# Layout of the filter loads, queue assignment, norm by reciprocal square root, and E±O on VectorE in a spectral mixer kernel

## The chip, the cores and the metric

The kernel runs on one core of one Trainium2 chip. The metric is device time in microseconds (us), the median of several runs. Runs carry a state, fast or slow, and only fast runs are compared. The engines are called PE (TensorE; PEld is its weight load), DVE (VectorE), ACT (ScalarE), POOL (GpSimd) and SP (SyncE, which here only issues loads and stores). Line numbers such as L714 are those of the kernel that the profile belongs to, so the same operation has another number before and after.

## The reference, cut to what matters

```python
# x: 1 x 2048 x 512 bf16; w_r, w_i: 2048 x 257; w1: 2048 x 1376; w2: 1376 x 2048
h  = x + irfft2(rfft2(layernorm(x)) * (w_r + 1j * w_i))     # "A": a spectral filter
g  = layernorm(layernorm(h))                                # B norms its input again
u  = gelu(einsum("bsd,sf->bdf", g, w1) + b1)
y  = einsum("bdf,fs->bds", u, w2) + b2
out = h + transpose(y)
```

Both Fourier transforms are done as matmuls. The kernel runs through four stages: A, norm of x and the first transform over the rows (matmuls of X with F, the matrix F scaled by 1/std first, because the norm can be folded into the matrix); B, the filter in 16 chunks c (matmul with E, matmul with L, multiply P with the filter, matmul with H); C, the inverse transform in 16 blocks, each normed and at once fed into six of the eleven row tiles of the first layer, then the other five tiles; D, the second layer and the stores.

## The kernel before

The program is not written instruction by instruction. Every operation is entered with the pieces of memory that it reads and writes. A builder notes, per 32-byte cell of a partition's memory, who wrote and who read it, makes the dependencies from that, and a list scheduler then fixes the order on each engine. This is the function that turns an access into cells; `lo` is the tensor's place in a partition, `ap.ap` lists (step, count) per dimension, the first being the partition:

```python
CELL = 32
def cells_of(self, ap):
    lo = self.tensors[ap.tensor.name]
    esz = dt.size(ap.dtype)
    gran = CELL if lo < (1 << 20) else 256
    offs = np.array([int(ap.offset)], dtype=np.int64)      # <- includes start partition * pitch
    for step, n in list(ap.ap)[1:]:
        ...
    b = lo + offs * esz
    return np.unique(...)                                  # cell numbers
```

The filter loads: three pieces of the frequency range, each cut by component, real or imaginary row, and two more indices, 16 partitions each, half on SyncE's queue, half on GpSimd's; 52 loads in all:

```python
pieces = [(0, 8), (8, 18), (18, 32)]
for pi, (ta, tb) in enumerate(pieces):
    for comp, wsrc in enumerate((A_w_r, A_w_i)):
        q = "sp" if comp == 0 else "pool"
        ...  # for reim, j, sgn: p0 = 4 * j + 2 * sgn + reim
            dma(f"ld_w{comp}_{pi}_{p0}_{a}", q, W[p0:NP:8, a:b, comp, :], src, ...,
                group=f"W{pi}{q}", wgroup=f"W{pi}")
K.op("mk_eps", "dve", lambda e, eng: eng.memset(eps[:, 0:1], LN_EPS), outs=[eps[:, 0:1]], ...)
```

The norm and the inverse, cut:

```python
K.op(f"sd{g}", "act", ... activation(sd, var, ACT.Sqrt, bias=eps) ...)
K.op(f"rs{g}", "dve", ... reciprocal(rs, sd) ...)
K.op(f"fs{n2}_{s}", ("pool" if g < 7 else "dve"), ... FS[:, n2, 128*s:128*s+128] = F * rs * (1 - 2 s) ...)
...
# inverse block n2: E and O are the halves of eo; result is [E+O, E-O] through one matrix
eng.matmul(ps[:, bA, :] as 2 x 256, IF[:, 0, n2, :], E broadcast twice, start=True, stop=False)
eng.matmul(ps[:, bA, 0:256],   IF[:, 0, n2, :], O, start=False, stop=False)
eng.matmul(ps[:, bA, 256:512], IF[:, 1, n2, :], O, start=False, stop=True)     # IF[:, 1] = -IF[:, 0]
# then DVE: H = ps + X; ACT: square with accumulation, Sqrt; DVE: reciprocal, HH = (H + nm) * A2
```

## Time and profile before

| | |
|---|---|
| time, median of 3 | 176.13 us (175.13 to 176.43) |
| span in the profile | 174.4 us |
| stage A, to the first filter matmul | 49.78 us, of which VectorE is busy in none of the first 31.48 |
| stage B, filter | 26.10 us |
| stage C, inverse with the first six tiles (36.96), other five tiles (20.34) | 57.30 us |
| stage D | 41.2 us |

From the page of the kernel before, the busy shares in 40 slices of 4.36 us (a digit is tenths):

```profile
...
PE   0000000088858999685989889899999999999992
...
DVE  0000000788507786836453455510000333223331
...
POOL 7994000069630100000000000000000000000000
...
DMA  5999987000039999999400000000000011111011
...
```

The first seven slices show loads running at full tilt and no computing engine at work; GpSimd is busy only because its load issues count as work. The chain of waits, followed back from the last instruction (start us, length us, what), has this near its beginning:

```profile
...
0.74 2.70 DMA X<-in_A_x_dram
3.44 28.04 issue
31.48 0.08 DVE st L509
...
```

The first x tile landed at 3.44 us. Then follow 28.04 us of "issue", the name for time in which the engine waited for nothing that the profile could name. The timeline of the start (start, length, engine, line, operation, out<-in, count) shows what ran meanwhile:

```profile
...
1.27 13.98 POOL L459 DMA_DIRECT2D W<-in_A_w_i_dram  x26 [0.82 <-POOLq L825]
...
7.82 21.22 SPq L459 DMA_DIRECT2D W<-in_A_w_r_dram  x26
31.48 0.69 DVE L509 BATCH_NORM_STATS2 st<-X 128x6 f32<-128x512 bf16 x1 [31.48 <-issue]
31.50 0.06 DVE L499 MEMSET eps<- 128x1 f32 x1
...
```

The memset of `eps` needs no data at all and yet ran at 31.5 us. (The record of the first statistics starts 0.02 us before the memset's; by its operands it waits for x alone, which had landed at 3.44 us, so it seems to have stood behind the memset in VectorE's queue.) The operands in the trace say that the memset waits on a semaphore, and that this is the semaphore of the last group of SyncE's filter loads, whose last landing is at 31.45 us. SyncE issues those 26 loads in 21.22 us. What that holds up is told by the list of waits of the whole kernel (waiting engine, its tile and line, what it waits for: us in total, times, longest):

```profile
...
PE ps L535 <- POOL FS L521: 36.3, 3, 35.5
...
ACT junk L501 <- DVE eps L500: 27.9, 1, 27.9
...
```

The stages of the kernel before in the view by stretches (stretch, length, then busy us and count of instructions for PE, PEld, DVE, ACT, POOL, then granted TensorE clock, DMA share, GB/s):

```profile
...
0.00:49.78 49.78, 11.49 (x65) 7.57 (x65) 13.30 (x50) 11.28 (x18) 24.06 (x58) 1.00 0.55 149
49.78:75.88 26.10, 22.78 (x257) 18.88 (x257) 17.89 (x28) 19.44 (x36) 2.69 (x6) 1.00 0.97 371
75.88:112.84 36.96, 32.69 (x191) 17.71 (x196) 17.91 (x45) 23.16 (x61) 0.00 (x0) 1.00 0.25 81
...
```

In the inverse stage TensorE is busy 32.69 of 36.96 us. In the last two stretches it is busy 20.23 of 20.34 and 37.86 of 41.22 us.

### The profile page before, as it was taken

To read this page: it belongs to the slowest core of one execution; us is meant where nothing else is said; L and a number is where in the kernel's file an instruction comes from. 1 tells how busy PE (TensorE), PEld (TensorE's weight loads), DVE (VectorE), ACT (ScalarE), POOL (GpSimd) and SP (SyncE) were. 2 spreads that over 40 slices of the span, in tenths; PEclk is the share of its full clock that TensorE was granted. 3 is DMA by queue.
4 is the path that set the end of the run, shared out by engine and by line. 5 is a ranking of instruction groups with operands and counts; after the bars stand their busy time and mean duration, and the time that the engine had idled before them with its cause. 6 is when DMAs were issued, how large, how long until landed. Compare 5 with 4: busy or idle time off the path is not lost.

```text
span 174.4 us, 2045 instructions
## 1 busy us (share of the span) xinstructions
PE 125.1 (72%) x775; PEld 78.9 (45%) x784; DVE 62.4 (36%) x142; ACT 63.2 (36%) x130; POOL 26.7 (15%) x64
## 2 busy tenths in 40 slices
PE   0000000088858999685989889899999999999992
PEld 0000000055637978553545445444446666666661
DVE  0000000788507786836453455510000333223331
ACT  2000000136778787647467664695121000000000
POOL 7994000069630100000000000000000000000000
PEclk9999999999999999999999999999999999999999
DMA  5999987000039999999400000000000011111011
GB/s 136 311 315 283 274 202 167 14 0 0 2 96 294 406 421 411 421 357 305 192 0 0 0 0 4 0 0 0 0 4 0 30 60 60 60 64 57 33 60 62
DMA packets 13322, 22.23 MB, mean 127 GB/s; under 512 B 1792, under 2 KB 9120, under 8 KB 13184
## 3 DMA queue, kind: packets, MB, share of 16 engines
q1 hardware_dynamic: 11392, 19.21, 32.3%
q0 software_dynamic: 1200, 2.11, 5.1%
q10 hardware_dynamic: 720, 0.79, 1.5%
q8 instruction: 6, 0.10, 0.2%
q14 instruction: 4, 0.03, 0.1%
HBM read 20.00 MB, written 2.10 MB: 127 GB/s over the span
## 4 chain that ended last, share of the span: by engine, by line
PE 62%; issue 18%; ACT 8%; DVE 8%; DMA 2%; POOL 1%; DVEq 0%
PE ps L751 20%; PE ps L714 19%; PE ps L535 5%; PE ps L623 4%; PE ps L589 4%; PE ps L680 3%; DVE H L695 2%; ACT Y L546 2%; PE ps L689 2%; PE ps L572 2%; ACT SQ L698 2%; DMA X<-in_A_x_dram 2%; ACT Xsb L598 1%; PE ps L757 1%; DVE HH L706 1%
## 5 line engine op out<-in xcount | busy, mean ns | idle before, releaser
L714 PE MATMUL ps<-HH,W 128*128 128x512 bf16 (+1 forms) x171 | 40.8, 379 | 4.1 <-DVE A L704 2.1
L535 PE MATMUL ps<-FS,X 128*128 128x256 bf16 x64 | 11.5, 357 | 36.7 <-POOL FS L521 36.3
L751 PE MATMUL ps<-GT,W 128*128 128x512 bf16 (+1 forms) x162 | 35.7, 379 | 0.2
L751 PEld LDWEIGHTS ps<-GT,W 128*128 128x128 bf16 (+1 forms) x165 | 23.8, 144 | 11.9
L763 DVE SCALAR_TENSOR_TENSOR OUT<-ps,B2f,H 128x512 bf16<-128x512 f32 x16 | 12.0, 751 | 44.6 <-PE ps L751 24.4
L714 PEld LDWEIGHTS ps<-HH,W 128*128 128x128 bf16 (+1 forms) x176 | 17.0, 100 | 20.9 <-issue 4.0
L535 PEld LDWEIGHTS ps<-FS,X 128*128 128x128 bf16 x64 | 7.6, 125 | 40.3 <-POOL FS L521 37.3
L509 DVE BATCH_NORM_STATS2 st<-X 128x6 f32<-128x512 bf16 x16 | 10.2, 669 | 31.5 <-issue 31.5
L698 ACT ACTIVATE SQ<-H,nm 128x512 bf16<-128x512 bf16 x16 | 11.5, 717 | 9.4 <-DVE H L695 9.4
L459 POOL DMA_DIRECT2D W<-in_A_w_i_dram x26 | 14.0, 551 | 0.8 <-POOLq L825 0.8
L695 DVE TENSOR_TENSOR H<-ps,X 128x512 bf16<-128x512 f32 x16 | 10.9, 689 | 7.7 <-PE ps L692 7.7
L521 POOL TENSOR_SCALAR FS<-F,rs 128x128 bf16<-128x128 bf16 x28 | 9.9, 372 | 21.3 <-DVE mv L511 21.1
L605 DVE TENSOR_TENSOR P<-Xsb,W 128x1024 bf16<-128x1024 bf16 x16 | 10.6, 685 | 5.5 <-ACT Xsb L598 5.4
L684 ACT ACTIVATE EO<-ps 128x512 bf16<-128x512 f32 x16 | 9.1, 585 | 5.1 <-PE ps L680 5.1
L733 ACT ACTIVATE GT<-ps,B1f 128x512 bf16<-128x512 f32 (+1 forms) x11 | 6.9, 695 | 10.9 <-PE ps L714 10.8
L598 ACT ACTIVATE Xsb<-ps 128x512 bf16<-128x512 f32 x16 | 9.4, 596 | 3.1 <-PE ps L589 3.1
L589 PE MATMUL ps<-Bsb,Lm 128*128 128x256 bf16 x64 | 9.6, 274 | 1.2 <-ACT Bsb L576 1.2
L623 PE MATMUL ps<-Hm,P 128*128 128x128 bf16 x128 | 9.3, 219 | 1.5 <-DVE P L605 1.3
L501 ACT ACTIVATE junk<-eps 128x1 f32<-128x1 f32 x1 | 0.2, 202 | 27.9 <-DVE eps L500 27.9
L546 ACT ACTIVATE Y<-ps 128x1024 bf16<-128x1024 f32 x8 | 8.1, 1022 | 5.2 <-PE ps L535 5.1
L638 DVE CAST TT<-ps 128x512 bf16<-128x512 f32 x12 | 7.9, 689 | 5.3 <-PE ps L623 5.3
L680 PE MATMUL ps<-GD,TT 128*128 128x256 bf16 x64 | 9.3, 273 | 0.7 <-ACT TT L637 0.7
(37 smaller groups left out, 97.8 us busy)
## 6 DMA issues: line engine op xcount, KB each, us to landing
W<-in_B_w_dram SPq DMA_DIRECT2D x8, 688.0 KB, 13.4
W<-in_B_w_dram SPq DMA_DIRECT2D x10, 512.0 KB, 17.3
out_dram<-OUT SPq DMA_DIRECT2D x16, 128.0 KB, 1.7
X<-in_A_x_dram SPq DMA_DIRECT2D x7, 256.0 KB, 10.2
IF<-c_IF SPq DMA_DIRECT2D x1, 1024.0 KB, 6.0
W<-in_A_w_i_dram POOLq DMA_DIRECT2D x8, 112.0 KB, 6.8
W<-in_A_w_r_dram SPq DMA_DIRECT2D x8, 112.0 KB, 3.1
W<-in_A_w_i_dram POOLq DMA_DIRECT2D x8, 80.0 KB, 6.3
```

Source lines behind the costliest of these rows:

```text
L459: return eng.dma_start(dst, src)
L535: r = eng.matmul(ps[:, b, 256 * u:256 * u + 256].rearrange("p (a b) -> p a b", a=2), X[:, n2, 128 * t:128 * t + 128], fr if t < 2 else fa, ...
L546: return eng.activation(dst, src, ACT.Copy)
L589: r = eng.matmul(ps[:, b, 256 * h:256 * h + 256], Lm[:, v, m, :], Bs[:, 256 * m:256 * m + 256], start=(h == 0 and m == 0), stop=(h == 1 an ...
L598: return eng.activation(dst, src, ACT.Copy)
L623: r = eng.matmul(o, P[:, h, m, par::2], Hm[:, v, m, :], start=(c % 2 == 0 and h == 0 and m == 0), stop=(c % 2 == 1 and h == 1 and m == 1), ...
L680: r = eng.matmul(o, TT[:, q, n2, par, :], GD[:, par, q, :], start=(i == 0), stop=(i == 3), skip_group_check=True)
L695: K.op(f"h{n2}", "dve", lambda e, eng: eng.tensor_tensor(H[:, n2, :], ps[:, bA, :], X[:, n2, :], ALU.add), ins=[ps[:, bA, :], X[:, n2, :]] ...
L698: K.op(f"sq{n2}", "act", lambda e, eng: eng.activation(sq[:, :], H[:, n2, :], ACT.Square, bias=nm[:, n2, 0:1], accum_out=s2t[:, n2, 0:1]), ...
L714: return eng.matmul(ps[0:Mt, bank, :], W1[:, n2, 128 * t:128 * t + Mt], HH[:, n2, :], start=(n2 == 0), stop=(n2 == 15), skip_group_check=True)
L751: r = eng.matmul(ps[:, b, :], W2[t][0:Kt, n2::16], GT[0:Kt, t, :], start=(t == 0), stop=(t == NFT - 1), skip_group_check=True)
L763: K.op(f"fin{n2}", "dve", lambda e, eng, n2=n2, b=b: eng.scalar_tensor_tensor(OUT[:, n2, :], ps[:, b, :], B2f[:, n2:n2 + 1], H[:, n2, :], ...
```

## The change

Its intent: filter loads of 32 partitions each (28 in place of 52), all on SyncE behind x, so that GpSimd is free for scaling F; F stored with its negative beside it (256 columns) so that one scaling per block does; F's loads on ScalarE's and GpSimd's queues; 1/std in one ScalarE activation (Abs_reciprocal_sqrt) in place of Sqrt and a VectorE reciprocal; statistics of blocks 1 and 3 on ScalarE; in the inverse, E+O and E-O on VectorE for the last 13 blocks and one matmul in place of three, while the first three blocks add x through an identity matrix on TensorE. The matrices L, H, F are permuted to suit the new row order. And, unannounced, the dependency builder is altered: the offset is taken modulo the partition's size, PSUM gets one cell per bank, and two readers of one bank are put in order. The core of the diff:

```diff
 def cells_of(self, ap):
-    gran = CELL if lo < (1 << 20) else 256
-    offs = np.array([int(ap.offset)], dtype=np.int64)
+    gran = CELL if lo < (1 << 20) else PSUM_BANK
+    pitch = int(np.prod(list(ap.tensor.shape)[1:])) * dt.size(ap.tensor.dtype) // esz
+    offs = np.array([int(ap.offset) % pitch], dtype=np.int64)
...
-            wv = wsrc.rearrange("(k2 r) k -> k2 r k", r=NP)
-            q = "sp" if comp == 0 else "pool"
-            (16 partitions: W[p0:NP:8, a:b, comp, :], 52 loads)
+            wv = wsrc.rearrange("(q r) k -> q r k", r=64)
+            (32 partitions: W[2 * ss + reim:NP:4, a:b, comp, :], 28 loads, all on "sp")
...
-    for g in range(4): ld_F on "act", 4 blocks of 128 columns each
+    for g in range(8): ld_F on "act" if g < 2 else "pool", 2 blocks of 256 columns each
...
+    ACT_STATS = (1, 3)                      # x**2 and x summed on ScalarE for these blocks
-    sd = Sqrt(var + eps) on act; rs = reciprocal(sd) on dve; FS in two halves of 128
+    rs = Abs_reciprocal_sqrt(var + eps) on act; FS in one piece of 256
...
+    for lo, hi in ([(0, 2)] if g < 6 else [(0, 1), (1, 2)]):    # last two copies into Y: act and dve
...
-    three matmuls (512 + 256 + 256 columns) per inverse block
+    n2 < 3:  identity matmul of X, then the three
+    n2 >= 3: sd_[:, 0:256] = E + O, sd_[:, 256:512] = E - O on dve; one matmul of 512
```

## The prediction

> **What bounds the kernel now.** The chain of waits begins with 28.04 us of "issue" (3.44 to 31.48 us). The first x tile landed at 3.44 us, yet VectorE starts nothing until 31.48, and TensorE, ScalarE and GpSimd then wait for it (waits: TensorE 35.5 us, ScalarE 27.9). The trace's operands show why: the first VectorE instruction, the memset of eps, which needs no data, waits on the semaphore of the last filter piece, whose last landing is at 31.46. I read this as a false dependency. The dependency builder takes a slice's offset without removing its start partition, so filter slices starting at partition 1 to 7 appear to lie over other tiles, eps among them. The diff's least advertised line, the offset modulo the partition pitch, removes it.
>
> Stages (busy time in stretches): norm and first transform 31.5-49.8 (18.3 us), filter 49.8-75.9 (26.1), inverse plus first matmul 75.9-112.8 (36.9, TensorE busy 32.7), then two TensorE-bound stages to 174.4 (61.6).
>
> **Costs of the change, by stage.**
>
> 1. Start. The norm starts at about 3.5 us instead of 31.5, now under the loads. x and the doubled F are 3.15 MB; at the 0.31 MB/us of the early slices they land by about 12.5 us. VectorE needs 0.8 us per block (0.66 statistics overlapping 0.17 aggregation) for 14 blocks, plus the F scalings given to it (0.25 us for 128 columns now, estimate 0.3 for 256). Two blocks go to ScalarE, which delays the first transform to about 7 us. TensorE there runs cold (213 ns from matmul to matmul, later 109; the Trainium skill, "TensorE: Matmul & The Clock Gate", Part 1, gives half clock until some 3.4 us of activity; the trace agrees in size), 0.83 us a block, about VectorE's pace. So the stage ends near 19 us, not 49.8: about 31 us won. GpSimd's 14.0 us of filter issues were hidden behind the false wait.
>
> 2. Filter stage: same work, 26 us. Its data become the danger: 4.2 MB of filter in 512 B rows, 28 issues on SyncE at 0.6-0.8 us, landing about 20, 25 and 31 us by piece; the multiplies need them at about 21.5, 27 and 34. I expect no large wait.
>
> 3. Inverse stage: 13 blocks replace matmuls of 512+256+256 columns (0.44 us start to end of issue) by one of 512 (0.22): 2.8 us of TensorE less; three identity matmuls add 0.66. VectorE adds two 256-wide additions (estimate 0.25 us each) per block and loses the 0.16 us reciprocals and a hop. Block latency grows to about 4 us, so part is lost in waits. Net about 2.4 us won. Abs_reciprocal_sqrt replaces Sqrt one for one: I expect two table loads as now (1.28 us each). The skill, "ScalarE: Activation LUTs", Table sets, says cheap functions are in every set; were Square not, every block would pay that.
>
> 4. Last stages unchanged. Loads of W1 and W2 queue behind the filter (from about 30 us), landing about 35-60, ahead of need (47 and 100).
>
> **Prediction: 143 us** (176.1 - 30.8 - 2.4), 8 in 10 between 139.5 and 148. Faster by over 2%: 0.98; within: 0.01; slower: 0.01.
>
> **Right if** VectorE's first work is at 3-4 us; the first filter matmul at 18-20.5; filter stage 25-28 us; inverse stage 33-36; rest 61.6.
>
> **Wrong if** another false wait remains; the third filter piece lands after 34 us (multiplies waiting for DMA); the x loads are slowed by the F and filter traffic; ScalarE reloads tables; or the inverse stage stalls on the longer chain.

## The result, and the profile after

The changed kernel takes 144.92 us (median of 4, 143.80 to 145.36) against 176.28 us of the kernel before in the same rounds. The ratio of the means of their fast runs is 0.8229, 95% interval 0.8158 to 0.8301. Ratios in this text are always such: the mean time of one kernel's fast runs over that of the other's of the same rounds, so not quite the quotient of the medians. The measured time lies within the predicted range of 139.5 to 148, 1.9 us above the 143.0. The busy shares in the slices, from the page of the changed kernel:

```profile
...
PE   0059767899996897899999999999999999999991
...
DVE  0469762777788209777777710000032323232322
...
POOL 7238504220000000000000000000000000000000
...
DMA  4999799999999999930000000000011111111111
...
```

The slices are now 3.57 us long. VectorE works from the first slice on, and the loads run beside the work. The timeline of the start of the changed kernel:

```profile
...
0.79 0.06 DVE L498 MEMSET eps<- 128x1 f32 x1 [0.79 <-PEq L861]
...
3.53 0.69 DVE L523 BATCH_NORM_STATS2 st<-X 128x6 f32<-128x512 bf16 x1 [2.56 <-DMA X<-in_A_x_dram]
...
7.88 3.98 SPq L468 DMA_DIRECT2D W<-in_A_w_r_dram  x6
...
8.48 1.89 PE L548 MATMUL ps<-FS,X 128*128 128x256 bf16 x8 [8.48 <-POOL FS L534]
...
```

The memset runs at 0.79 us and the first statistics at 3.53 us, as soon as x is there. TensorE's first matmuls start at 8.48 us, while SyncE has only just begun to issue the filter loads (7.88 us). The stages of the changed kernel in the view by stretches, with the columns as before:

```profile
...
0.00:21.99 21.99, 9.95 (x65) 6.68 (x66) 13.30 (x40) 13.27 (x27) 10.61 (x27) 1.00 0.88 268
21.99:48.08 26.09, 22.77 (x257) 18.85 (x257) 17.89 (x28) 19.44 (x36) 2.81 (x6) 1.00 1.02 364
48.08:81.29 33.21, 31.59 (x171) 16.69 (x172) 21.10 (x56) 23.72 (x61) 0.00 (x0) 0.95 0.43 158
...
```

Beside the lines shown of before: stage A 49.78 to 21.99 us (27.8 won), B 26.10 to 26.09, the inverse stage 36.96 to 33.21 (3.75 won), the rest 61.6 both times. The last number before the DMA share is the granted clock: 0.95 in the inverse stage, which was 1.00 before. That is looked into below. One caution for this column: the clock records begin only at 13.78 us in this trace and at 44.14 us in that of before, and the view prints 1.00 ahead of them. TensorE was not at full pace there: the matmuls of the first transform start 213 ns apart up to these times and 109 ns apart after them. The end of stage A, from the chain of waits:

```profile
...
18.94 0.29 ACT rs L530
19.23 1.89 ACT Y L560 x3
21.12 0.02 issue
21.15 0.70 DVE Y L561
21.85 0.14 issue
21.99 0.61 PE ps L589 x4
...
```

After the last 1/std is known (19.23 us), three copies into Y on ScalarE take 1.89 us, and VectorE's copy of block 15 starts only when they are done. The reader should ask why it waits for ScalarE at all.

The steady part of the inverse stage, from the same kernel's chain of waits (start, length, what):

```profile
...
65.72 1.08 PE ps L748 x5
66.80 0.44 PE ps L702 x4
67.23 0.21 PE ps L748
67.45 0.22 PE ps L724
67.66 1.08 PE ps L748 x5
...
```

TensorE alone, with no other engine in the chain: 6 matmuls of the first layer (L748), four of the inverse's first half (L702), one of its second (L724), 1.95 us a block. Before, the chain passed through VectorE and ScalarE there, for instance in these lines of TensorE's timeline of the kernel before (the bracket gives the idle time ahead of the instruction and what ended it; 0.44 us waiting for VectorE's HH, 0.17 us for ScalarE's EO):

```profile
...
95.75 0.60 PE L680 MATMUL ps<-GD,TT 128*128 128x256 bf16 x4
96.79 1.04 PE L714 MATMUL ps<-HH,W 128*128 128x512 bf16 x4 [0.44 <-DVE HH L706]
...
100.37 0.39 PE L689 MATMUL ps<-EO,IF 128*128 128x512 bf16 x1 [0.17 <-ACT EO L684]
```

### The profile page after: what moved, and what is told of

Read it like the earlier page. It is cut to its first block, busy times and chain, and to the rows that moved or that the text cites. A ratio compares the mean times of both kernels' runs of the same rounds, so it can differ in the third digit from the quotient of the medians.

```text
span 142.9 us, 1989 instructions
## 1 busy us (share of the span) xinstructions
PE 122.9 (86%) x761; PEld 77.1 (54%) x761; DVE 65.7 (46%) x142; ACT 65.7 (46%) x139; POOL 13.4 (9%) x32
## 4 chain that ended last, share of the span: by engine, by line
PE 76%; ACT 8%; DVE 6%; issue 5%; POOL 3%; POOLq 0%
PE ps L748 27%; PE ps L785 25%; PE ps L702 5%; PE ps L640 5%; PE ps L606 5%; ACT Y L560 3%; POOL F L468 2%; PE ps L548 2%; PE ps L589 2%; PE ps L724 2%; ACT Xsb L615 2%; PE ps L791 2%; ACT Bsb L593 1%; ACT SQ L730 1%; POOL FS L534 1%
## 5 line engine op out<-in xcount | busy, mean ns | idle before, releaser
L748 PE MATMUL ps<-HH,W 128*128 128x512 bf16 (+1 forms) x176 | 42.0, 379 | 1.0 <-DVE HH L736 0.9
L785 PEld LDWEIGHTS ps<-GT,W 128*128 128x128 bf16 (+1 forms) x165 | 23.8, 144 | 11.9
L748 PEld LDWEIGHTS ps<-HH,W 128*128 128x128 bf16 (+1 forms) x176 | 17.4, 100 | 19.5 <-issue 1.7
L548 PE MATMUL ps<-FS,X 128*128 128x256 bf16 x64 | 9.9, 320 | 10.3 <-POOL FS L534 10.2
L730 ACT ACTIVATE SQ<-H,nm 128x512 bf16<-128x512 bf16 x13 | 9.4, 722 | 6.7 <-DVE H L726 6.7
L726 DVE TENSOR_TENSOR H<-ps,X 128x512 bf16<-128x512 f32 x13 | 9.0, 691 | 6.2 <-PE ps L724 6.1
L523 DVE BATCH_NORM_STATS2 st<-X 128x6 f32<-128x512 bf16 x14 | 9.1, 672 | 5.7 <-DMA X<-in_A_x_dram 5.7
L702 PE MATMUL ps<-GD,TT 128*128 128x256 bf16 x64 | 10.6, 300 | 1.3 <-ACT TT L654 0.7
L589 PE MATMUL ps<-E,Y 128*128 128x256 bf16 x64 | 8.3, 272 | 1.8 <-DVE Y L561 1.8
L702 PEld LDWEIGHTS ps<-GD,TT 128*128 128x128 bf16 x64 | 6.7, 107 | 5.4 <-ACT EO L706 1.0
L593 ACT ACTIVATE Bsb<-ps 128x512 bf16<-128x512 f32 x16 | 8.7, 603 | 1.5 <-PE ps L589 1.5
L640 PEld LDWEIGHTS ps<-Hm,P 128*128 128x128 bf16 x128 | 7.8, 98 | 2.7 <-DVE P L622 1.8
```

The lines of the kernel that those rows point to most:

```text
L548: r = eng.matmul(ps[:, b, 256 * u:256 * u + 256].rearrange("p (a b) -> p a b", a=2), X[:, n2, 128 * t:128 * t + 128], fr if t < 2 else fa, ...
L589: r = eng.matmul(o, Y[:, k, c, :], E[:, k, :].rearrange("p (h r) -> p h r", h=2), start=(i == 0), stop=(i == 3), skip_group_check=True)
L593: K.op(f"Be{c}", "act", lambda e, eng: eng.activation(Bb[c % 3][:, :], ps[:, b, :], ACT.Copy), ins=[ps[:, b, :]], outs=[Bb[c % 3][:, :]], ...
L640: r = eng.matmul(o, P[:, h, m, par::2], Hm[:, v, m, :], start=(c % 2 == 0 and h == 0 and m == 0), stop=(c % 2 == 1 and h == 1 and m == 1), ...
L702: r = eng.matmul(o, TT[:, q, n2, par, :], GD[:, par, q, :], start=(i == 0), stop=(i == 3), skip_group_check=True)
L730: K.op(f"sq{n2}", "act", lambda e, eng: eng.activation(sq[:, :], hsrc, ACT.Square, bias=nm[:, n2, 0:1], accum_out=s2t[:, n2, 0:1]), ins=[h ...
```

## The experiments

Twelve runs were made, e12 being the changed kernel once more; all gave correct results. Stages are read from each one's profile. "Stage C" is here the time from the first inverse matmul to the first matmul of the second layer, a boundary that is easy to find in every trace (57.30 us before, 53.55 after).

| kernel | time, us | stage A | B | C |
|---|---|---|---|---|
| before | 176.0 to 176.7 | 49.78 | 26.10 | 57.30 |
| after | 144.92; again 144.54 | 21.99; 21.88 | 26.09 | 53.55; 53.47 |
| e1 before, offset modulo pitch | 157.95 | 31.43 | 26.10 | 57.08 |
| e2 after, without the modulo | 169.51 | 47.86 | 26.09 | 53.64 |
| e3 after, three matmuls | 148.86 | 22.23 | 26.09 | 57.80 |
| e4 after, 16-partition loads | 155.13 | 22.24 | 37.61 | 51.98 |
| e5 after, Sqrt and reciprocal | 146.71 | 23.59 | 26.09 | 55.67 |
| e6 after, cells of 16 bytes | 143.29 | 22.68 (a slow run) | 26.10 | 53.86 |
| e7 after, half the filter on GpSimd | 147.69 | 24.69 | 26.08 | 53.85 |
| e8 after, all statistics on VectorE | 142.61 | 20.70 | 27.20 | 52.20 |
| e9 after, unread matmuls | 143.71 | 21.24 | 26.10 | 51.98 |
| e10 three edits | 140.91 | 20.78 | 25.71 | 51.98 |
| e11 three edits and unread matmuls | 140.59 | 19.86 | 25.72 | 51.97 |

One caution for reading stage A: it hangs on when x lands, and that differs from run to run. The third x load was complete at 6.49 us in the profile of the changed kernel and at 9.12 us in that of e6. Three runs whose work in stage A is the changed kernel's (e4, e9, e12) have 22.24, 21.24 and 21.88 us there, so differences of half a microsecond in this column mean little. The profiled run of e5 also needs care; see there.

### e1 and e2: the modulo alone, and everything but the modulo

Theory: the start was held by a false dependency, and the modulo in the dependency builder removed it. Rival: the start was held by the loads themselves, and the new load layout freed it.

The arithmetic of the false dependency can be done from the memory layout. A partition of W holds 32 x 2 x 256 bf16 = 32,768 bytes, and W starts at byte 61,952. The third piece is entries 18 to 31, each 1,024 bytes. Its load that starts at partition 3 was entered as bytes 61,952 + 3 x 32,768 + 18 x 1,024 = 178,688 to 193,024, and `eps` stands at byte 191,168, in the same range as the tiles of the statistics. So the memset "overwrites" what a filter load wrote and must wait for it; the loads of the piece share one semaphore count, so it waits for all of them.

```diff
 (e1, applied to the kernel before; e2 is the same edit taken out of the changed kernel)
-        offs = np.array([int(ap.offset)], dtype=np.int64)
+        pitch = int(np.prod(list(ap.tensor.shape)[1:])) * dt.size(ap.tensor.dtype) // esz
+        offs = np.array([int(ap.offset) % pitch], dtype=np.int64)
```

> The kernel before with one thing changed: the dependency builder takes a slice's offset modulo the partition pitch, so the memset of eps no longer waits for the last filter piece. Theory (false wait): VectorE starts at about 3.5 us instead of 31.5. GpSimd still issues its 26 filter loads (14.0 us) mixed with the 28 scalings (10 us), so the first filter matmul comes at 27 to 29 us instead of 49.8, and the time falls by about 21 us, to 153 to 157. Rival (the loads themselves hold the start, by traffic or by queue order): VectorE still starts near 31 us and the time stays at 176.

> The changed kernel with the modulo taken out again. The built program then again has the eps memset wait for the last filter group. Theory: VectorE starts at about 31.2 us, when the last filter piece lands, the first filter matmul comes at 46 to 49 us, and the time is 169 to 173. Rival (the wider filter loads and the freed GpSimd are what bring the start forward): the time stays within 3 us of 145.

Measured: e1 157.95 us (156.81 to 158.90), ratio to the kernel before 0.8981 (0.8924 to 0.9039); e2 169.51 us (169.04 to 171.30), ratio 0.9626 (0.9577 to 0.9675). The memset of e1 ran at 0.81 us and the first work of e2 on VectorE at 30.71, with the last landing of the filter at 30.68. The theory holds both ways and the rival falls. The wider loads do not bring the start forward by themselves: stage A of e2 is only 1.92 us shorter than that of before.

e1 came out 1 us slower than its range, with its first filter matmul at 31.43 us instead of 27 to 29. GpSimd's timeline in e1 shows what bound it next:

```profile
...
10.37 1.42 POOL L522 TENSOR_SCALAR FS<-F,rs 128x128 bf16<-128x128 bf16 x4 [2.62 <-DVE mv L512]
11.74 3.21 POOL L460 DMA_DIRECT2D W<-in_A_w_i_dram  x6
14.98 1.42 POOL L522 TENSOR_SCALAR FS<-F,rs 128x128 bf16<-128x128 bf16 x4
16.35 4.39 POOL L460 DMA_DIRECT2D W<-in_A_w_i_dram  x8
20.77 7.03 POOL L522 TENSOR_SCALAR FS<-F,rs 128x128 bf16<-128x128 bf16 x20
...
```

GpSimd's load issues stand between its scalings of F: the last 20 of 28 scalings begin at 20.77 us, when the last issue is done, and end at 27.80. That is the part of the change that the intent names, and it pays only once the false wait is gone. The times add up in this way: the modulo alone wins 18.1 us (176.0 to 157.95), everything else alone 6.5 us (to 169.5), both together 31.4 us in the rounds of the result (31.8 in those of e12). Some 7 us belong to neither alone.

### e4 and e7: 16-partition loads, and half the filter on GpSimd

```diff
 (e4)
-    dma(..., "sp", W[2 * ss + reim:NP:4, a:b, comp, :], src, ...)
+    for hf in range(2):
+        dma(..., "sp", W[2 * ss + reim + 4 * hf:NP:8, a:b, comp, :], src[hf::2], ...)
 (e7)
-    dma(..., "sp", W[...], src, ..., group=f"W{pi}", ...)
+    dma(..., ("sp", "pool")[comp], W[...], src, ..., group=f"W{pi}{comp}", ...)
```

> The changed kernel with each filter load of 32 partitions cut into two of 16, all on SyncE: 56 issues instead of 28, the same bytes. Theory (SyncE's issue time of about 0.65 us each sets when the filter lands): the last piece lands near 46 us instead of 31, the tenth multiply waits about 8 to 11 us, time 152 to 156. Rival (bandwidth sets it, issues hardly matter): the last piece lands within 2 us of 31 and, with 5.9 us of slack before the tenth multiply, the time stays at 145.

> The changed kernel with the imaginary half of the filter (14 of 28 loads) back on GpSimd's queue. Theory: GpSimd's issues (about 0.55 us each) stand between its scalings of F again, the first transform waits for them, and the first filter matmul comes 1.5 to 4 us later; time 146.5 to 149. Rival (the filter lands earlier with two issuers and nothing else changes): 145 or less.

Measured: e4 155.13 us (154.68 to 156.44), ratio 0.8836; its filter stage takes 37.61 us instead of 26.09. Its list of waits in the filter stage has a line that no such list of the changed kernel has:

```profile
...
DVE P L623 <- DMA W<-in_A_w_i_dram: 11.9, 3, 4.4
...
```

VectorE's multiply waits for the filter three times, 11.9 us in all. SyncE's timeline in e4, its first and last group of filter issues, shows why:

```profile
...
8.12 7.71 SPq L468 DMA_DIRECT2D W<-in_A_w_r_dram  x12
...
39.69 5.87 SPq L468 DMA_DIRECT2D W<-in_A_w_i_dram  x8
...
```

The 56 issues last from 8.12 to 45.56 us, 0.67 us each, each group lands 1.7 to 2.9 us after its last issue, and from 22.24 to 38 us the DMA engines are busy only 0.51 to 0.53 of the time. The Trainium skill, "DMA: Bandwidth & Descriptors", section "Issuing engines are not separate DMA queues", says that several issuing engines only save issue time, "which is usually small relative to the DMA itself". For loads of 16 partitions the issue time, not the bandwidth, set when the filter landed. With 32 partitions the 28 issues end at 27.2 us, the last piece lands at 31.12 us, and its first user runs at 36.99 us, so 5.9 us are to spare.

e7 took 147.69 us (147.03 to 147.78), ratio 0.8398, as expected in size. (Against the kernel before, the record classes this run as unclear, although its interval, 0.8346 to 0.8449, lies far below 1; the reason is not on record.) Its profile shows three causes that this run does not separate. GpSimd's issues stand between its scalings again (its third group of scalings begins at 15.22 us), and x lands later because the filter on the second queue shares the DMA engines with it: the last x load is complete at 16.34 us instead of 13.06. The second effect agrees with the skill's statement in the same section that queues interleave on the same engines. The third is the clock: it was halved from 16.96 to 20.38 us, inside stage A, where 16 matmuls ran 213 instead of 109 ns apart.

### e3: three matmuls per inverse block

```diff
 (for blocks 3 to 15 of the changed kernel)
-    DVE: sd_ = [E + O, E - O];  PE: one matmul of 512 with sd_
+    PE: matmul 512 (E twice, start), matmul 256 (O, +IF), matmul 256 (O, -IF, stop)
```

> The changed kernel with blocks 3 to 15 of the inverse computed as before, by three matmuls of 512+256+256 columns in place of E+O and E-O on VectorE and one matmul of 512. Theory (this stage is bound by TensorE): 13 x 0.22 us = 2.8 us come back, time about 147.7, inverse stage 36. Rival (the stage was won by the shorter norm chain and the earlier first blocks): less than 1 us comes back.

Measured: 148.86 us (148.31 to 149.19), ratio 0.8463 (0.8425 to 0.8502), so 3.9 us slower than the changed kernel by the medians (the two ran in different calls), and stage C 4.25 us longer. The direction of the theory holds; the size is larger. The rival falls: with the three matmuls back, stage C is 57.80 us, and even without the half-clock stretch (about 1.5 us, see e9) it would be within about 1 us of the 57.30 of before, although the other edits of the inverse are still in. Counting between the starts of the third and the last HH, 13 blocks take 2.42 us each in e3 against 2.11 in the changed kernel (1.95 in its steady part) and 2.53 before. TensorE's own work in e3 is 1.95 + 0.22 = 2.17 us a block. The rest is waiting, and it shows up once every second block in the chain of waits of e3:

```profile
...
66.69 0.69 DVE H L728
67.38 0.33 DVE HH L738
67.71 0.14 issue
67.85 1.46 PE ps L750 x6
...
```

So TensorE's saved 0.22 us per block is 2.8 of the 4.25 us, and the other 1.4 us is a wait for VectorE (H and HH) that the order found by the scheduler has with three matmuls and does not have with one. The schedule is static and comes from estimated durations. Whether another order would avoid that wait with three matmuls was not tried, so this part is measured but not explained further.

### e5: Sqrt and reciprocal

```diff
-    rs = Abs_reciprocal_sqrt(var + eps)               # act
+    sd = Sqrt(var + eps)  # act;   rs = reciprocal(sd)  # dve     (both norms, and the warm-up)
```

> The changed kernel with both norms computed as before, Sqrt on ScalarE and a reciprocal on VectorE, in place of Abs_reciprocal_sqrt. Theory: the hop to VectorE lies on the chain of the first stage (about 0.2 us per pair of blocks, only the last counts) and of the first inverse blocks; the steady inverse stage is bound by TensorE. So 0.2 to 0.8 us slower than 144.9. Rival (the shorter norm chain is a main part of the inverse stage's 3.75 us): 2 us or more slower.

Measured: 146.71 us (146.11 to 148.51; one run slow), ratio 0.8357 (0.8300 to 0.8414), about 2 us slower than the changed kernel and outside the expected 0.2 to 0.8. Its profiled run took 148.22 us and has the half-clock stretch described under e9, while four of its five other runs took 146.11 to 146.93 us at a clock of 0.997 or more. So the stages of this profile, A 1.6 us and C 2.1 us longer than the changed kernel's, add up to more than the 2 us between the medians. The number is the rival's, but the run does not prove the rival's reason: the other durations made the scheduler order the inverse's VectorE and TensorE work differently (in its trace the later HH follow each other at steps of 1.43 to 3.15 us, in the changed kernel's mostly at 1.95), and the chain of e5 has stretches of waiting for ScalarE at 61.35 and 73.05 us that the changed kernel has not. So "Sqrt and reciprocal, with the schedule that results, cost 2 us" is shown; how much of it is the hop itself is not. Both kernels load two activation tables, 1.28 us each. The fear in the prediction of more table loads was unfounded.

### e6: cells of 16 bytes

Blocks 14 and 15 lie in Y as neighbouring pieces of 16 bytes (8 bf16). With cells of 32 bytes the two copies seem to write the same cell, and the builder orders VectorE's behind ScalarE's: a second false wait, which the change brought with it when it split the last copies between the engines.

```diff
-CELL = 32
+CELL = 16
+    (VectorE's copies kept behind its last scaling by an explicit dependency, so that all engine orders stay the same)
```

> The changed kernel with the dependency builder's cell of 16 bytes instead of 32 (engine orders unchanged). The copies of blocks 14 and 15 into Y are 16-byte pieces side by side, so with 32-byte cells VectorE's copy of block 15 waits for ScalarE's of block 14 as if they overlapped. Theory (a second false wait, new in the changed kernel): VectorE's last copy starts near 20.3 instead of 21.15, and the first filter matmul comes 0.4 to 0.8 us earlier; time 144.2. Rival (ScalarE's own last copy is the limit): less than 0.2 us.

Measured: 143.29 us, ratio 0.8145 (0.8098 to 0.8192). The changed kernel had 0.8194 (0.8148 to 0.8240), so by time alone the difference of about 0.9 us is not certain. The chain is clear, though. Its profiled run was a slow one, so only the shape and not the start of the stage is compared. The end of stage A in the chain of waits of e6:

```profile
...
20.45 0.29 ACT rs L530
20.75 1.89 ACT Y L560 x3
22.64 0.05 issue
22.68 0.62 PE ps L589 x4
...
```

From the end of ScalarE's copies to the first filter matmul it is 0.04 us instead of 0.87. The expectation for VectorE was right, and the rival's point was right as well: ScalarE's three copies (1.89 us) are now the end of the stage. A measure that does not hang on x says the same: from the start of the last aggregation to the first filter matmul it is 3.27 us in the changed kernel and in e12, and 2.45 us in e6 and in e10, which has the same edit.

### e8: all statistics on VectorE

```diff
-    ACT_STATS = (1, 3)
+    ACT_STATS = ()
```

> The changed kernel with the statistics of blocks 1 and 3 on VectorE again instead of ScalarE. ScalarE's way takes two passes and four small steps, so the first scaling waits until 7.95 us though x1 landed at 4.84. Theory: the first transform matmul comes at about 6.5 us instead of 8.5, but the end of the stage is set by VectorE's pace from the third x load on; first filter matmul within 0.6 us, time 144.3 to 145. Rival A (the late start is what costs): 1.5 us or more faster. Rival B (VectorE is overloaded by two more blocks): 0.7 us or more slower.

Measured: 142.61 us (142.40 to 145.43; one run slow), ratio 0.8113 (0.8065 to 0.8160), about 1.5 us faster than the changed kernel's 0.8194 (0.8148 to 0.8240). The intervals still overlap by a hair, and the calls differ, but no fast run of either kernel falls among the other's. The first transform matmul comes at 7.04 us, half a microsecond later than expected, but the stage ends at 20.70, not within 0.6 us of 22. The expectation was wrong: VectorE had idle time while x arrived, so two more blocks cost it little: 14 of the 16 blocks' statistics are done at 15.48 us in e8, 12 of VectorE's 14 at 15.84 in the changed kernel. There VectorE then stands idle for 0.82 us in front of a scaling of F that needs ScalarE's 1/std, which itself stood behind a copy into Y (15.43 to 16.45 us); in e8 that scaling starts without a wait. The last statistics were aggregated at 17.45 us instead of 18.72. The size is near that of rival A, but the late start is not what the trace shows as the cause. How much of the 1.3 us in stage A is the edit is less sure, since e9, with the changed kernel's stage A, had 21.24.

Part of the win was lost again: e8's filter stage is 1.1 us longer. The trace shows the clock halved from 21.61 to 25.02 us.

### e9 to e12: the half-clock stretch, and a better version

The changed kernel's trace has one stretch of 3.41 us at half clock, at 47.91 to 51.33 us. The view by stretches for the 3.41 us before it and for it:

```profile
...
44.50:47.91 3.41, 1.57 (x20) 0.96 (x17) 2.90 (x5) 1.17 (x3) 0.00 (x0) 1.00 1.02 420
47.91:51.33 3.42, 3.25 (x14) 2.11 (x15) 0.00 (x0) 1.78 (x4) 0.00 (x0) 0.50 1.02 418
...
```

In the 3.41 us before, TensorE was busy 1.57 us. It waits there for the multiply of the fifteenth chunk, since VectorE first makes two copies of TT. The Trainium skill, "TensorE: Matmul & The Clock Gate", Part 1, describes a free-running window of 3413 ns after which an idle TensorE gets half the clock; the length agrees to the digit. But the busy share in the window does not settle it: in the trace of the kernel before, TensorE was busy 1.34 us of the window from 78.28 to 81.69 us (windows counted in steps of 3.413 us from the first clock record), and the clock stayed at 1.00 after it. The edits:

```diff
 (e9) the changed kernel, plus matmuls into a free PSUM bank that nobody reads:
+    fill(6 x 512 columns) before chunk 15's matmul with H;  fill(2 x 512) before the first inverse matmul
 (e10) the changed kernel, three edits, no fill:
-    ACT_STATS = (1, 3)
+    ACT_STATS = ()
-CELL = 32
+CELL = 16
-    eng_ = ("dve" if (par == 0 or pair % 2 == 0) else "act") if c < 15 ...
+    eng_ = ("dve" if (par == 0 or (pair % 2 == 0 and pair < 6)) else "act") if c < 15 ...
      (and, as in e6, VectorE's copies into Y kept behind its last scaling)
 (e11) e10 and fill(4) before the first filter matmul, fill(1) and fill(3) at the two places of e9
```

> The changed kernel itself, unaltered, as the yardstick for the other three of this call on the same chip. Expected 144 to 145.5, in most runs with a granted clock near 0.988, which is one stretch of 3.41 us at half clock, at the start of the inverse stage.

> The changed kernel with eight matmuls added whose result nobody reads: six of 512 columns where TensorE waits for the multiply of the fifteenth filter chunk, two before the first inverse matmul. Theory (TensorE was idle over half of the 3.41 us before, so its clock was halved for the next 3.41 us): granted clock 1.0 in most runs, no half-clock stretch at the start of the inverse stage, 0.7 to 1.5 us faster than the unaltered kernel of this call. Rival (the half-clock stretch is not tied to TensorE's idle time there, or costs nothing as the stage's start is bound elsewhere): within 0.3 us or slower.

> The changed kernel with three edits: all statistics on VectorE, dependency cells of 16 bytes, and one of the two copies of TT of the seventh pair of chunks moved from VectorE to ScalarE, so that VectorE multiplies the fifteenth chunk sooner. Theory: the first filter matmul comes near 20 us (22.0 in the changed kernel), the filter stage is 0.5 us shorter unless a half-clock stretch falls into it; 141 to 142.5. Rival (the gains of the statistics and of the cells overlap): no faster than 142.6.

> The three edits of the former run and unread matmuls in the idle stretches of TensorE: four before the first filter matmul, one before the fifteenth chunk's, three before the first inverse matmul. Theory: granted clock 1.0 in most runs and 0.8 to 1.5 us faster than the former run, 140 to 141.5. Rival: the added matmuls delay real ones and the time is the same or worse.

All four ran on one chip.

| kernel | median, us | ratio to before, 95% | granted clock near 0.988, of 6 runs |
|---|---|---|---|
| e12, changed kernel again | 144.54 | 0.8194 (0.8148 to 0.8240) | 5 |
| e9 | 143.71 | 0.8170 (0.8119 to 0.8222) | 3 |
| e10 | 140.91 | 0.8000 (0.7955 to 0.8045) | 1 |
| e11 | 140.59 | 0.7981 (0.7938 to 0.8024) | 0 |

e9 is half a success. Its profiled run has no half-clock stretch and a stage C of 51.98 us instead of 53.47, with the same engine work. That trace holds no clock records at all, so its clock of 1.0 shows nothing by itself; but the first inverse matmuls start 109 ns apart in it and 213 ns apart in the changed kernel, so the pace confirms it. Other fast traces with the same work in stage C say the same: 51.97 to 52.20 us without the stretch there (e4, e8, e10, e11), 53.47 to 53.85 with it (the changed kernel, e2, e7, e12). So the stretch costs about 1.5 us of the stage where it occurs. But three of its six runs still have the lower clock, the times of e9 and e12 overlap, and the one run of e12 with a clock of 1.0 took 144.57 us, in the middle of its others. Where the stretch fell in those runs is not known, since one trace per kernel is kept.

e10 and e11 beat both kernels. Dividing ratios, e10 takes 0.8000 / 0.8194 = 0.976 of the changed kernel's time; the two intervals do not touch. e10 gains 1.1 us in stage A, 0.4 us in B (the moved copy lets the fifteenth multiply start sooner) and 1.5 us in C (no half-clock stretch in its profiled run, though it has no fill). e11 against e10 is undecided: 0.3 us between medians, overlapping intervals. That the shorter wait for the fifteenth multiply is what spares e10 the half clock is an inference.

## Why the prediction was right or wrong, point by point

- **"I read this as a false dependency"**: right, and shown by e1 and e2. The change's title does not name its most valuable part.
- **"About 31 us won" at the start**: the mechanism was right, the size off. Stage A ended at 21.99, not 19 us, so 27.8 us were won. The first transform came at 8.48 us, not 7, but that was not the main thing. The sum left out the tail: after the last 1/std there are three ScalarE copies (1.89 us) and a VectorE copy with its handover (0.87 us), 2.8 us together. 0.83 us of it is the new false wait of e6. The prediction had also taken over the choice of ScalarE for two blocks' statistics; e8, without it, had a stage shorter by 0.5 to 1.5 us, depending on which run of the changed kernel's stage A it is set against. So the mark for the first filter matmul under "right if" (18 to 20.5 us) was missed, and one of the fears under "wrong if", another false wait, came true in small.
- **"GpSimd's 14.0 us of filter issues were hidden behind the false wait"**: right for the kernel before; e1 shows them coming out of hiding once the wait is gone.
- **Filter stage "same work, 26 us", "no large wait"**: right, 26.09 us. Landings were foretold at 20, 25 and 31 us and came at 17.59, 24.07 and 31.12; the needs were foretold at 21.5, 27 and 34 and came at 24.55, 30.42 and 36.99.
- **"Net about 2.4 us won" in the inverse stage**: too small; 3.75 us was won, and it would have been about 5.3 us without the half-clock stretch. The failed step is "block latency grows to about 4 us, so part is lost in waits". The opposite happened: before, a block took 2.53 us against 2.17 of TensorE work, and after it takes 1.95 us with TensorE never waiting in the steady part. Over the whole stretch TensorE's idle time fell from 4.27 to 1.62 us. e3 puts 4.25 us of stage C on E±O with its schedule. What e5 puts on the activation, 2.1 us by its slower profiled run, is less sure, and the two overlap.
- **"Two table loads as now"**: right.
- **"W1 and W2 landing about 35-60, ahead of need"**: nearly right; the last landed at 64.48 us, long before its use at about 102.
- The clock was foreseen for the first transform only, and there the prediction's trace does not agree with the 3.4 us of activity that it took from the skill: half pace lasted 8.7 us from the first matmul in the kernel before (35.47 to 44.14, TensorE busy in 8.0 of them), and 5.3 us in the changed kernel (8.48 to 13.78, busy in 4.6). The half-clock stretch in the inverse stage (about 1.5 us) was in no term.
- Sum: 3.0 us too much in stage A, 1.35 us too little in the inverse stage, which leaves 1.65 us of span; foretold 143.0, measured 144.9 us. That two misses of opposite sign cancel to this extent was luck; the false wait, which carries most of the sum, was not.

## What to carry to other kernels

When an engine idles at the start and the profile only says "issue", read the semaphore that its first instruction waits on and ask whether it could need that data; if a memset waits for a load that does not touch its memory, look for a fault in the dependency tracking before you blame the loads. Apply one part of a change alone, and all but that part: here the parts won 18.1 and 6.5 us alone and 31.4 together, so neither number alone tells what a part is worth. When a new split puts two engines on neighbouring bytes, check that the tracker's grain is as fine as the split.

## What the Trainium skill lacked or had wrong

- "DMA: Bandwidth & Descriptors", "Issuing engines are not separate DMA queues", calls issue time usually small relative to the DMA. Here 56 loads of 16 partitions (1 to 14 rows of 512 bytes to a partition, so 8 to 112 KiB) took SyncE 0.67 us apiece, 37.4 us in all, and delayed the kernel by 10 us (e4); 32-partition loads of the same bytes took 28 issues and left 5.9 us of slack. Its size rule, 64 KB, does not reach most of these loads (40 of the 56 are of 64 KiB or more); a rule for the size at which issue binds is lacking.
- "TensorE: Matmul & The Clock Gate", Part 1, gives the window (3413 ns, seen here exactly) and names idle windows, or in one kernel frequent short idles, as the cause. It gives no share of activity below which the clock is halved. Here a window in which TensorE was busy 1.57 of 3.41 us, not idle, was followed by a halved one, about 1.5 us of loss in the stage, while one with 1.34 us busy (the kernel before, 78.28 to 81.69 us) was not; and a clock near 0.988 came in 5 of 6 runs of one kernel and 1 of 6 of another.
- "ScalarE: Activation LUTs", Table sets, does not list the set with Abs_reciprocal_sqrt. The runs show that Copy and Square work beside it without a reload: two table loads in the whole kernel, 1.28 us each, as with Sqrt.
- No page that was looked up here warns that a load's start partition can leak into a dependency tracker's byte offset; the cost was 18.1 us for that alone (e1).
